# Pooling V for the last twenty head pairs on GpSimd, from a second load of V, and the FFN blocks dealt out four and five to a slot

## The chip, the cores and the metric

The kernel runs on one core of a Trainium2 chip. The core has five engines with a queue of instructions each: TensorE (PE, matrix multiplies, with PEld for its weight loads), VectorE (DVE), ScalarE (ACT), GpSimd (POOL) and SyncE (SP, which here does nothing but issue transfers). Sixteen DMA engines move the data. The metric is the time of one execution on the device, in microseconds (us); the median of several runs is compared.

## What is computed

Local and pooled attention are added, and the sum goes through a gated feed-forward network (FFN). Q, K and V have 8 batches, 8 heads, 576 tokens and 64 columns.

```python
q_d = q.reshape(B, H, Sd, factor, D).mean(axis=3)      # factor = 4, Sd = 144
k_d = k.reshape(B, H, Sd, factor, D).mean(axis=3)
v_d = v.reshape(B, H, Sd, factor, D).mean(axis=3)
out_d = sm_attn(q_d, k_d, v_d)                         # softmax attention over 144 pooled tokens
out_up = np.repeat(out_d, factor, axis=2)
mask = np.abs(pos[:, None] - pos[None, :]) < factor    # a band of seven keys
scores = np.where(mask, scale * np.matmul(q, k.transpose(0, 1, 3, 2)), -1e9)
attn = softmax(scores)
x = (out_up + np.matmul(attn, v)).transpose(0, 2, 1, 3).reshape(B * S, H * D)
return (np.maximum(x @ w_gate, 0.0) * (x @ w_val)) @ w_out   # 4608 x 512, FFN width 1536
```

The change is about `v_d`, the mean of V over each group of four tokens.

## The kernel before

Work on attention goes by **pairs** of heads, 32 of them (`p`), four to a batch. The FFN goes by **chunks** of 512 tokens, nine of them (`c`): twelve h blocks each (eight matmuls into two PSUM banks, a Relu on ACT, a product `g` on DVE, lines 532 to 548) and four y blocks (twelve matmuls into one bank, a copy `y_sb` on ACT, lines 550 to 562). `ffn` (line 571) lists the blocks in order, with the y blocks of chunk c-1 between the h blocks of chunk c: h h h y, and so on; in the first chunk an empty entry stands where a y would be. `ffn_do` (line 580) takes the next entry, but an h block of chunk c is only taken once all pairs of the batches that it reads are done (`made`, at least four times the number of those batches); otherwise it returns with nothing done.

The order of all instructions is written out by hand in `slot(n)` (line 604), which is called for n from -2 to 33. In slot n the pair n has its scores, pair n-1 or n-2 its outputs, and later pairs are loaded and cast; `quota` says how many FFN blocks are dealt into the slot: none before slot 4, three up to slot 13, four from slot 14 on. What is left of `ffn` after the last slot runs as a tail. Every engine works through its own instructions in this order.

The first twelve pairs (`NPE = 12`) are transposed by PE. The last twenty are transposed by DMA: `turn_qk` and `turn_a` on SP's queue (lines 239 and 456). For them a slot has these steps, in program order:

- SP: `turn_a(n-1)` (L459 and L460, which make `at` and `adt`), `turn_qk(n+2)` (L244, twice), then `load` of pair n+5 (Q and K in rows of 256 bytes, L178, into `nat`; V twice into `vst`, L185), then `store_y` (L567).
- PE: `scores(n)` (L313, `s_ps`), `scores_d(n)` (L330, `d_ps`), `pool_v(n)` (L344 and L353, `v_ps`), an FFN block, `outputs(n-2)` (L487 `u_ps`, L504 `o_ps`), and three more FFN blocks.
- DVE: mask (L364), maximum and subtraction (L386, L387, `sm`), the pooled maximum (L370, L371), then the products `g`, the sums and weights of pair n, and `add_x(n-2)` (L521), which adds `u_ps` and `od` into `xT`.
- ACT: `copy_vd(n)` (L397), the exponentials (L418, L406), the Relus, `od` (L512), a cast of Q (L224), `y_sb` (L561).
- POOL: `pool_qk(n+1)` (L300 `t`, L303 `qkd`), `weights_d(n)` (L447 `adn`, two multiplications), and for pair n+3 the cast of K (`cast_qk_pool`, L226) and of V (`cast_v`, L237).

V is loaded so that its tokens lie by windows: a tile `vst` of 112 partitions, rows 0 to 47 and 64 to 111, with 18 windows of 64 columns; it is cast into `v16`. The outputs of the local attention multiply this tile. `pool_v` makes the pooled V from the same tile with a constant matrix `pool_sb` that holds 0.25: eight matmuls (L344) accumulate the first 128 groups of four tokens of both heads into `vp[:, 0:2]`, and four smaller ones (L353) give the last 16 groups, in `vp[:, 2:4]`. `copy_vd` casts the whole to `vd`, which `outputs` multiplies with `adt`.

All of `s_ps`, `v_ps`, `h_ps`, `u_ps`, `o_ps` and `y_ps` come from one pool of six PSUM banks that are given out in turn (`bank`, line 138); `d_ps` has two of its own. The SBUF pools that the change touches are `v16` (7 buffers), `sm` (2) and `vst` (3 fixed tiles, `v_t[p % NV]`).

Of the kernel before, what the change touches and what calls it, by code (L numbers as in the profile page):

```python
# [10 lines left out]
FP32 = mybir.dt.float32  # L11
FP16 = mybir.dt.float16
AF = mybir.ActivationFunctionType
ALU = mybir.AluOpType
# [27 lines left out]
def _dap(t_ap: bass.AP, extra_off: int, dims) -> bass.AP:  # L42
    return bass.AP(tensor=t_ap.tensor, offset=t_ap.offset + extra_off, ap=list(dims))
# [3 lines left out]
def kernel(  # L47
# [10 lines left out]
    nc = tc.nc  # L58
    B, H, S, D = q.shape
# [11 lines left out]
    NPE = 12  # L71
# [16 lines left out]
    def pool(name, bufs):  # L88
        return ctx.enter_context(tc.tile_pool(name=name, bufs=bufs))
# [7 lines left out]
    en_t = [cpool.tile([96, 12, 64], FP16, name=f"en{i}") for i in range(NA)]  # L97
    ad_t = [cpool.tile([80, 6, 128], FP16, name=f"adn{i}")[:, 0:5] for i in range(NA)]
    p_nat = pool("nat", 4)
    p_16 = pool("h16", 3)  # L100
    p_at = pool("at", 2)
    p_adt = pool("adt", 2)
# [11 lines left out]
    nc.scalar.activation(out=warm, in_=warm, func=AF.Exp)  # L114
    nc.scalar.dma_start(mask_sb, mask_dr)
    nc.scalar.dma_start(pool_sb, pool_dr)
    p_v16 = pool("v16", 7)
    p_t1 = pool("t1", 1)
    p_qkd = pool("qkd", 2)
    p_sm = pool("sm", 2)  # L120
    p_e = pool("e", 2)
    p_st = pool("st", 4)
    p_ed = pool("ed", 2)
    p_vd = pool("vd", 4)
    p_od = pool("od", 2)
    psum = ctx.enter_context(tc.tile_pool(name="psum", bufs=6, space=bass.MemoryType.PSUM))
    psum_d = ctx.enter_context(tc.tile_pool(name="psum_d", bufs=2, space=bass.MemoryType.PSUM))
# [10 lines left out]
    def bank(shape, name, dt=FP32):  # L138
        return psum.tile(shape, dt, name=name, tag="bank")


    def load_h_weights(i):
        cols = slice(384 * i, 384 * i + 384)
        for src, dst in ((w_gate, wg_sb), (w_val, wv_sb)):
            nc.gpsimd.dma_start(
                dst[:, :, cols],
                _dap(src, 384 * i, [[DF, 128], [128 * DF, 4], [1, 384]]),
            )

    def load_y_weights(i):  # L150
        nc.gpsimd.dma_start(
            wo_sb[:, 3 * i : 3 * i + 3, :],
            _dap(w_out, 3 * i * 128 * DM, [[DM, 128], [128 * DM, 3], [1, DM]]),
        )


    st = {}

    def load(p):
        off = 2 * p * S * D  # L160
        nat = p_nat.tile([96, 2, 768], FP32, name="nat", tag="nat")
        if p < NPE:


            t = nat.rearrange("p a c -> p (a c)").rearrange("p (b h c) -> p b h c", b=3, h=2)
            for src, r0, r1, blk, g0 in (
                (q, 0, 96, 0, 0),
                (q, 0, 48, 1, 96),
                (k, 48, 96, 1, 0),
                (k, 0, 96, 2, 48),  # L170
            ):
                nc.sync.dma_start(  # L172
                    t[r0:r1, blk],
                    _dap(src, off + 4 * g0 * D, [[4 * D, r1 - r0], [S * D, 2], [1, 4 * D]]),
                )
        else:
            for i, src in ((0, q), (1, k)):
                nc.sync.dma_start(  # L178
                    nat[:, i].rearrange("p (h j d) -> p h j d", h=2, j=6),
                    _dap(src, off, [[D, 96], [S * D, 2], [96 * D, 6], [1, D]]),  # L180
                )
        vst = v_t[p % NV]

        def win(rows, lo, par, w, nw):
            nc.sync.dma_start(  # L185
                vst[64 * par + lo : 64 * par + lo + rows, w : w + nw, :],
                _dap(
                    v,
                    off + (32 * (2 * w + par) - 3 + lo) * D,
                    [[D, rows], [64 * D, nw], [1, D]],  # L190
                ),
            )


        if p == 0:
            win(48, 0, 0, 1, NW - 1)
            win(45, 3, 0, 0, 1)
        else:
            win(48, 0, 0, 0, NW)
        if p == NP - 1:  # L200
            win(48, 0, 1, 0, NW - 1)
            nc.vector.memset(vst[96:VR, NW - 1, :], 0.0)
            win(35, 0, 1, NW - 1, 1)
        else:
            win(48, 0, 1, 0, NW)
        st[p] = dict(nat=nat, vst=vst)


    def cast_qk(p, i):
# [18 lines left out]
    def cast_qk_act(p):  # L228
        cast_qk(p, 0)
# [108 lines left out]
    def pool_v(p):  # L338
        s = st[p]
        v16 = s["v16"]  # L340
        s["vp"] = vp = bank([128, 4, D], "v_ps")
        v2 = v16.rearrange("p (h l) d -> p h l d", h=2)
        for l in range(8):
            nc.tensor.matmul(  # L344
                out=vp[:, 0:2, :],
                lhsT=pool_sb[:, 128 - 16 * l : 256 - 16 * l],
                rhs=v2[:, :, l, :],
                start=(l == 0),
                stop=(l == 7),
            )  # L350
        for c in range(2):
            for h in range(2):
                nc.tensor.matmul(  # L353
                    out=vp[64 * h : 64 * h + 64, 2 + c, :],
                    lhsT=pool_sb[:, 128 - 32 * c : 192 - 32 * c],
                    rhs=v2[:, h, 8, :],
                    start=True,
                    stop=True,
                )
# [34 lines left out]
    def copy_vd(p):  # L394
        s = st[p]
        s["vd"] = p_vd.tile([128, 4, D], FP16, name="vd", tag="vd")
        nc.scalar.copy(out=s["vd"], in_=s.pop("vp"))  # L397

    def exp_d(p, h):
        s = st[p]  # L400
        if h == 0:
            s["ed"] = p_ed.tile([80, 4, S // 4], FP16, name="ed", tag="ed")
            s["sd"] = p_st.tile([80, 4], FP32, name="sd", tag="sd")
        for c in range(2):
            i = 2 * h + c
            nc.scalar.activation(  # L406
                out=s["ed"][:, i, :],
                in_=s["dp"][h][:, c, :],
                func=AF.Exp,
                scale=SCALE / 16.0,  # L410
                bias=s["nb"][:, i : i + 1],
                accum_out=s["sd"][:, i : i + 1],
            )
# [150 lines left out]
    def store_y():  # L564
        while ysb:
            row, y_sb = ysb.pop(0)
            nc.sync.dma_start(_dap(out, row * DM, [[DM, 128], [1, DM]]), y_sb)  # L567
# [12 lines left out]
    def ffn_do():  # L580
        if ffn:
            t = ffn[0]
            if t and t[0] == "h" and made[0] < 4 * (min((t[1] + 1) * TCH - 1, NTOK - 1) // S + 1):
                return
            ffn.pop(0)
            if t:
                (ffn_h if t[0] == "h" else ffn_y)(t[1], t[2])
# [5 lines left out]
    def at_stage(p, *fs, pe=None):  # L593
        if 0 <= p < NP and (pe is None or pe == (p < NPE)):
            for f in fs:
                f(p)
# [5 lines left out]
    loaded = [0]  # L602

    def slot(n):
        quota = 0 if n < 4 else 3 if n < 14 else 4
        at_stage(n - 1, turn_a, pe=False)
        at_stage(n + 2, turn_qk, pe=False)
        while loaded[0] < min(NP, n + (5 if n < NPE - 2 else 6)):
            load(loaded[0])
            loaded[0] += 1  # L610
        store_y()
        at_stage(n, scores, scores_d)
        at_stage(n - 1, turn_en_pe, pe=True)
        at_stage(n, pool_v, mask_l, shift_l, copy_vd, exp_l, max_d)
        if n == 0:
            cast_qk_act(1)
        at_stage(n + 2, cast_qk_pool, pe=True)
        if n + 2 < NPP:
            at_stage(n + 2, cast_v, pe=True)
        at_stage(n + 1, pool_qk, pe=False)  # L620
        if n < 4 or n >= NPE:
            at_stage(n + 1, turn_qk_pe, pe=True)
        if quota > 1:
            ffn_do()
        if 4 <= n < NPE:
            at_stage(n + 1, turn_qk_pe, pe=True)
        at_stage(n - 1, turn_ad_pe, pe=True)
        at_stage(n, lambda p: exp_d(p, 0))
        at_stage(n - 1, outputs, pe=True)
        at_stage(n - 2, outputs, pe=False)  # L630
        at_stage(n, sums, weights_l)
        at_stage(n - 1, x_stage, pe=True)
        at_stage(n - 2, x_stage, pe=False)
        at_stage(n, lambda p: exp_d(p, 1))
        if n != -1:
            at_stage(n + 2, cast_qk_act, pe=True)
        if quota:
            ffn_do()
        if n + 2 >= NPP:
            at_stage(n + 2, cast_v, pe=True)  # L640
        at_stage(n + 1, pool_qk, pe=True)
        at_stage(n, weights_d)
        at_stage(n + 3, cast_qk_act, cast_qk_pool, cast_v, pe=False)
        if 1 <= n < 5:
            load_h_weights(n - 1)
        elif 5 <= n < 9:
            load_y_weights(n - 5)
        if quota > 2:
            ffn_do()
        if quota > 3:  # L650
            ffn_do()

    with tc.manual_schedule():
# [35 lines left out]
```

## Time and profile before

| What | us |
|---|---|
| median of three runs | 412.59 (412.29 to 413.22) |
| the profiled execution | 413.64 |
| its span, from the first to the last instruction | 411.9 |
| PE busy in the span | 388.7 |
| L344, the eight pooling matmuls, 256 in all (mean 234 ns each as recorded, overlapping) | 21.9 |
| POOL busy | 167.8 |
| waits of PE in the slots from 130.48 to 251.52 | none |
| DMA: 59.02 MB, of which HBM read | 42.63 MB |

A line of the chain of waits has the start, the length and the work; the chain is followed back from the last instruction, so its pieces are the time that set the end. A line of a timeline has the start, the length, the engine, the line of the code, the operation, output and inputs, and in brackets how long the engine stood idle before it and for whom it waited. In the table by stretches the columns are the stretch, its length, the busy times of PE, PEld, DVE, ACT and POOL with the number of instructions, the TensorE clock that was granted (1.00 is full), the mean busy share of the sixteen DMA engines (packets overlap, so it can exceed 1), and GB/s. In the page's forty slices each digit is a busy share in tenths. SPq is SP's queue of transfers; the length there is the time that issuing took. Lengths of one engine's instructions overlap a little, since the next starts before the last has drained.

### The profile page before, as it was taken

Reading aid. Unit: us, or ns where it says so; the run is one execution under the profiler, and the core shown is the slowest. Engines: PE = TensorE matmul, PEld = TensorE weight load, DVE = VectorE, ACT = ScalarE, POOL = GpSimd, SP = SyncE. Lnnn points to the kernel's source line nnn. Section 1 sums busy time; section 2 is a strip of 40 time slices with the busy share of each in tenths; the row PEclk is TensorE's granted clock in tenths of the full one; section 3 lists DMA queues with packets and bytes.
Section 4 is the critical chain, followed back from the end, with each engine's and each line's share of the span. In section 5 each row is a group of like instructions: output and inputs, shape, how many; then the busy total and the mean of one; then the engine's idle time right before and its main releaser. Section 6 shows DMA issues by size and latency. Waiting matters only on the chain.

```text
span 411.9 us, 11866 instructions
## 1 busy us (share of the span) xinstructions
PE 388.7 (94%) x4704; PEld 205.6 (50%) x4704; DVE 252.1 (61%) x639; ACT 208.2 (51%) x580; POOL 167.8 (41%) x212
## 2 busy tenths in 40 slices
PE   2699998898999999999999999999999999999996
PEld 2587455454555555455555555545554444444442
DVE  2789599878668777777777777777773232232220
ACT  3577578766665555555555555555442322322321
POOL 5587776655557544444444444444211000000000
PEclk9999999898999999999999999999999999999999
DMA  8999999968996999889989899766341100010012
GB/s 189 235 228 231 239 220 227 204 127 143 195 193 142 191 197 190 163 181 198 182 182 181 180 180 179 165 127 120 52 54 50 44 34 27 34 42 27 27 51 102
DMA packets 167261, 59.02 MB, mean 143 GB/s; under 512 B 149846, under 2 KB 162598, under 8 KB 167206
## 3 DMA queue, kind: packets, MB, share of 16 engines
q1 hardware_dynamic: 161030, 53.38, 64.3%
q0 software_dynamic: 5824, 4.72, 7.8%
q8 instruction: 37, 0.61, 0.7%
q10 hardware_dynamic: 352, 0.16, 0.2%
q14 instruction: 18, 0.15, 0.1%
HBM read 42.63 MB, written 9.44 MB: 126 GB/s over the span
## 4 chain that ended last, share of the span: by engine, by line
PE 77%; DMA 6%; DVE 6%; ACT 4%; SPq 3%; issue 2%; POOL 1%; ACTq 0%; POOLq 0%; DVEq 0%
PE h_ps L537 42%; PE y_ps L553 22%; DMA vst<-in_v_dram 5%; SPq L172 3%; PE v_ps L344 3%; PE o_ps L504 2%; PE s_ps L313 2%; PE u_ps L487 2%; DVE sm L387 2%; PE d_ps L330 1%; DVE s_ps L364 1%; DVE mx L386 1%; DMA nat<-in_k_dram 1%; ACT ed L406 1%; ACT r L545 1%
## 5 line engine op out<-in xcount | busy, mean ns | idle before, releaser
L547 DVE TENSOR_TENSOR g<-r,h_ps 128x512 f16<-128x512 f16 x108 | 74.0, 685 | 120.0 <-PE h_ps L537 116.7
L537 PE MATMUL h_ps<-xT,wg_sb 128*128 128x512 f16 x432 | 114.2, 387 | 0.2 <-DVE xT L521 0.2
L537 PE MATMUL h_ps<-xT,wv_sb 128*128 128x512 f16 x432 | 113.5, 386 | 0.0
L553 PE MATMUL y_ps<-wo_sb,g 128*128 128x512 f16 x432 | 99.5, 382 | 0.0
L447 POOL TENSOR_TENSOR adn<-ed,rd 80x512 f16<-80x512 f16 x64 | 41.1, 662 | 119.1 <-ACT h L224 72.3
L545 ACT ACTIVATE r<-h_ps 128x512 f16<-128x512 f32 x108 | 64.1, 593 | 39.3 <-PE h_ps L537 39.2
L537 PEld LDWEIGHTS <-wv_sb 128*128 128x128 f16 x432 | 42.9, 99 | 53.3 <-issue 3.7
L553 PEld LDWEIGHTS <-g 128*128 128x128 f16 x432 | 42.5, 99 | 51.9 <-issue 1.9
L537 PEld LDWEIGHTS <-wg_sb 128*128 128x128 f16 x432 | 38.3, 99 | 42.2 <-issue 2.7
L561 ACT COPY y_sb<-y_ps 128x512 f32<-128x512 f32 x36 | 21.1, 585 | 75.7 <-PE y_ps L553 75.7
L406 ACT ACTIVATE ed<-d_ps,nb 80x144 f16<-80x144 f32 x128 | 47.5, 381 | 0.0
L237 POOL CAST v<-vst 112x1152 f16<-112x1152 f32 x32 | 36.7, 1147 | 3.7 <-DMA vst<-in_v_dram 3.7
L300 POOL TENSOR_TENSOR t<-qkT 128x576 f32<-128x576 f16 x27 | 31.3, 1158 | 12.6 <-DVE qkT L269 8.9
L418 ACT ACTIVATE e<-sm 96x456 f16<-96x456 f32 x32 | 18.7, 583 | 30.8 <-DVE sm L387 30.7
L226 POOL CAST h<-nat 96x768 f16<-96x768 f32 x35 | 29.7, 847 | 5.0 <-DMA nat<-in_k_dram 5.0
L370 DVE TENSOR_REDUCE d_ps<-d_ps 80x2 f32<-80x288 f32 x64 | 28.9, 452 | 0.0
L397 ACT CAST vd<-v_ps 128x256 f16<-128x256 f32 x32 | 11.9, 373 | 32.8 <-PE v_ps L353 32.8
L521 DVE TENSOR_TENSOR xT<-u_ps,od 128x288 f16<-128x288 f32 x64 | 26.0, 446 | 3.0 <-ACT od L512 3.0
L224 ACT CAST h<-nat 96x768 f16<-96x768 f32 x29 | 24.2, 840 | 4.5 <-DMA nat<-in_k_dram 4.5
L387 DVE TENSOR_TENSOR sm<-s_ps,mx 96x228 f32<-96x228 f32 x64 | 25.1, 392 | 2.2
L406 ACT ACTIVATION_READ_ACCUMULATOR ed<-d_ps,nb 80x1 f32 x128 | 26.3, 205 | 0.0
L364 DVE TENSOR_TENSOR s_ps<-s_ps,mask_sb 96x228 f32<-96x228 f32 x64 | 22.1, 389 | 4.3 <-PE s_ps L313 4.3
(50 smaller groups left out, 367.0 us busy)
## 6 DMA issues: line engine op xcount, KB each, us to landing
vst<-in_v_dram SPq DMA_DIRECT2D x62, 216.0 KB, 5.0
out_dram<-y_sb SPq DMA_DIRECT2D x36, 256.0 KB, 2.2
nat<-in_q_dram SPq DMA_DIRECT2D x20, 288.0 KB, 3.4
nat<-in_k_dram SPq DMA_DIRECT2D x20, 288.0 KB, 4.3
nat<-in_q_dram SPq DMA_DIRECT2D x12, 192.0 KB, 6.3
nat<-in_k_dram SPq DMA_DIRECT2D x12, 192.0 KB, 5.3
wg_sb<-in_moe_w_gate_dram POOLq DMA_DIRECT2D x4, 384.0 KB, 7.7
wv_sb<-in_moe_w_val_dram POOLq DMA_DIRECT2D x4, 384.0 KB, 10.5
```

Of the source, the lines that this page charges most:

```text
L226: nc.gpsimd.tensor_copy(out=dst, in_=src)
L237: nc.gpsimd.tensor_copy(out=s["v16"], in_=s.pop("vst"))
L300: nc.gpsimd.tensor_tensor(out=t1, in0=qkv[:, :, :, 0], in1=qkv[:, :, :, 1], op=ALU.add)
L364: nc.vector.tensor_tensor(out=sp, in0=sp, in1=mask_sb, op=ALU.add)
L370: nc.vector.tensor_reduce(out=nbr, in_=s["dp"][h], axis=AX.X, op=ALU.max)
L387: nc.vector.tensor_tensor(out=sm[:, half, :], in0=sp, in1=mx[:, half, None].to_broadcast([96, 6, 38]), op=ALU.subtract,)
L406: nc.scalar.activation(out=s["ed"][:, i, :], in_=s["dp"][h][:, c, :], func=AF.Exp, scale=SCALE / 16.0, bias=s["nb"][:, i : i + 1], accum_o ...
L447: nc.gpsimd.tensor_tensor(out=o, in0=i, in1=rd[:, :, None].to_broadcast([80, 4, n]), op=ALU.mult)
L537: nc.tensor.matmul(out=h, lhsT=w[:, kk, bass.ts(jj, 128)], rhs=xT[:, kk, bass.ts(c, TCH)], start=(kk == 0), stop=(kk == 3),)
L545: nc.scalar.activation(out=r, in_=h1, func=AF.Relu)
L547: nc.vector.tensor_tensor(out=g, in0=r, in1=h2, op=ALU.mult)
L553: nc.tensor.matmul(out=y, lhsT=gts[c][jj][:, bass.ts(ty, 128)], rhs=wo_sb[:, jj, :], start=(jj == 0), stop=(jj == NJJ - 1),)
```

## The change

For the last twenty pairs, V is loaded a second time by `load_v4`: 128 partitions, each with a group of four tokens of both heads, in rows of 4 x 64 floats (1 KB). `sum_v4` adds the four tokens on POOL in two steps, and `copy_vd` scales the sum by 0.25 on ACT into `vd[:, 0:2]`. The eight matmuls of `pool_v` (L344) are left out for these pairs; the four of the last 16 groups stay, and their copy is an instruction of its own.

The other load of V is taken out of `load` into `load_v`. For the last twenty pairs it stands in slot n for pair n+4 instead of n+5, after the loads of Q and K and ahead of `load_v4`; `cast_v` moves from pair n+3 to n+2. The number of `v16` buffers goes from 7 to 5, of `sm` from 2 to 1; new are three buffers of `v4` and three of `s4`. From slot 14 on `quota` is four in even slots and five in odd ones.

```diff
+    p_v4 = pool("v4", 3)
...
-    p_v16 = pool("v16", 7)
+    p_v16 = pool("v16", 5)
...
-    p_sm = pool("sm", 2)
+    p_sm = pool("sm", 1)
...
+    p_s4 = pool("s4", 3)
...
+    def load_v4(p):
+        st[p]["v4"] = v4 = p_v4.tile([128, 2, 4 * D], FP32, name="v4", tag="v4")
+        nc.sync.dma_start(
+            v4, _dap(v, 2 * p * S * D, [[4 * D, 128], [S * D, 2], [1, 4 * D]])
+        )
+
+    def sum_v4(p):
+        s = st[p]
+        v4 = s.pop("v4")
+        s2 = v4[:, :, 0 : 2 * D]
+        nc.gpsimd.tensor_tensor(out=s2, in0=s2, in1=v4[:, :, 2 * D : 4 * D], op=ALU.add)
+        s["s4"] = p_s4.tile([128, 2, D], FP32, name="s4", tag="s4")
+        nc.gpsimd.tensor_tensor(
+            out=s["s4"], in0=s2[:, :, 0:D], in1=s2[:, :, D : 2 * D], op=ALU.add
+        )
...
-        for l in range(8):
+        for l in range(8) if p < NPE else ():
             nc.tensor.matmul(
                 out=vp[:, 0:2, :],
...
-        nc.scalar.copy(out=s["vd"], in_=s.pop("vp"))
+        vp = s.pop("vp")
+        if p < NPE:
+            nc.scalar.copy(out=s["vd"], in_=vp)
+        else:
+            nc.scalar.copy(out=s["vd"][:, 2:4], in_=vp[:, 2:4])
+            nc.scalar.activation(
+                out=s["vd"][:, 0:2], in_=s.pop("s4"), func=AF.Copy, scale=0.25
+            )
...
-        quota = 0 if n < 4 else 3 if n < 14 else 4
+        quota = 0 if n < 4 else 3 if n < 14 else 5 if n % 2 else 4
...
             load(loaded[0])
+            if loaded[0] < NPE:
+                load_v(loaded[0])
             loaded[0] += 1
+        at_stage(n + 4, load_v, load_v4, pe=False)
         store_y()
...
-        at_stage(n + 3, cast_qk_act, cast_qk_pool, cast_v, pe=False)
+        at_stage(n + 3, cast_qk_act, cast_qk_pool, pe=False)
+        at_stage(n + 2, cast_v, sum_v4, pe=False)
...
         if quota > 3:
+            ffn_do()
+        if quota > 4:
             ffn_do()
```

More of the change, by code (lines that the diff above doesn't have):

```diff
@@ L181, in load, with load_v @@
                 )
+        st[p] = dict(nat=nat)
+    def load_v(p):
+        off = 2 * p * S * D
         vst = v_t[p % NV]
@@ L205, in load @@
             win(48, 0, 1, 0, NW)
-        st[p] = dict(nat=nat, vst=vst)
+        st[p]["vst"] = vst
+    def load_v4(p):
[12 more added lines that the diff above has]
+        )
     def cast_qk(p, i):
```

## The prediction

> **What bounds the kernel now.** I read the page first, then the chain of waits, then single slots in the timelines.
>
> ```profile
> PE 388.7 (94%) x4704; PEld 205.6 (50%) x4704; DVE 252.1 (61%) x639; ACT 208.2 (51%) x580; POOL 167.8 (41%) x212
> PE   2699998898999999999999999999999999999996
> DMA  8999999968996999889989899766341100010012
> ```
>
> PE is full from about the twelfth slice on; up to slice 26 the DMA engines are nearly full too, and after that almost idle. So there are two candidates for the late slots, PE and transfers. The chain of waits from 241 to 252 us decides between them. It shows slot 25 (each pair has a slot, numbered here by its scores; T is the start of its `s_ps`, here 241.43):
>
> ```profile
> 241.43 0.36 PE s_ps L313 x36
> 241.79 0.25 PE d_ps L330 x4
> 242.04 0.55 PE v_ps L344 x8
> 242.59 0.18 PE v_ps L353 x4
> 242.77 1.83 PE h_ps L537 x8
> 244.60 0.39 PE u_ps L487 x36
> 245.00 0.37 PE o_ps L504 x8
> 245.37 1.83 PE h_ps L537 x8
> 247.20 2.59 PE y_ps L553 x12
> 249.79 1.73 PE h_ps L537 x8
> 251.52 0.36 PE s_ps L313 x36
> ```
>
> Every piece is PE and each begins where the last ended: a slot is PE work alone, 10.09 us. The slots from 130.48 on repeat this to 0.01 us. Its four blocks are h (1.73 us, 1.83 right after small matmuls) or y (2.59), and the tail after 320 us is the same blocks back to back. What PE loses in these slots comes off the end, if nothing else becomes late.
>
> **Part 1, eight pooling matmuls removed for pairs 12 to 31.** 0.55 us a slot in the row of L344; its four companions of L353 stay. Slots 13 to 31 are pure PE. In slot 12 the chain names DVE, but there PE runs s, d, v, then a y block (115.15 to 117.75); ACT stood idle 0.86 us before it copied that y (117.95) and made `adt` (118.44), for which `o_ps` waited 0.49 us. So v lies on the path there too. 20 x 0.55 = **-11.0 us**.
>
> **Part 2, five blocks in the odd slots.** By the block list, a slot runs what is ready, and chunk c waits until 4(c+1) pairs are done. That allows 29 blocks before slot 14 in both kernels, then 80 in before; in after the chunks 6 and 7 are not ready in slots 28/29 and 32/33, so 87, and the tail falls from 39 to 32 blocks. A block costs PE the same in a slot as in the tail: 0. Only the 0.10 us of an h after small matmuls falls away where a y or nothing stands there, up to ten times: between 0 and -1.0, taken as **-0.5**, the middle.
>
> **Part 3, banks that come free too late.** PE now comes to everything after v_ps 0.55 us sooner, while DVE's chain does not. The six PSUM banks go in turn (s s v h h u u o h h y ...), each to the sixth next user. The same slot on DVE:
>
> ```profile
> 243.16 0.39 DVE L387 TENSOR_TENSOR sm<-s_ps,mx 96x228 f32<-96x228 f32 x1
> 243.89 0.39 DVE L387 TENSOR_TENSOR sm<-s_ps,mx 96x228 f32<-96x228 f32 x1
> 247.48 0.81 DVE L521 TENSOR_TENSOR xT<-u_ps,od 128x288 f16<-128x288 f32 x2
> ```
>
> The second `sm` frees its bank for `o_ps` at 244.28 = T+2.85; `o_ps` starts at T+3.57 now and T+3.01 after: 0.1 us to spare after a hand-over of 0.05. Thin, but no wait. Where the second and third block of a slot are both h (slots 18 to 21, 26 to 31), the third's second half needs the bank of the first `u_ps`, free at 247.89 = T+6.46; PE comes at 0.79+1.83+0.76+1.83+0.86 = T+6.07. In 20, 21, 28, 30 and 31 the slot before ended in a y, so DVE has no g ahead of its masks and is some 0.2 earlier: a wait of 0.22 x 5 = **+1.1** (none to 0.44 each: 0 to +2.2). Slots 18, 19, 26 and 27 have a y first, which makes PE later, and wait nothing. Slot 29 has no first block at all (chunk 6 isn't ready): PE runs into the banks of `s_ps` (0.3) and then of `u_ps` (1.1): **+1.4** (0 to +2).
>
> **Part 4, GpSimd.** Two adds a pair over 128x256 and 128x128. L300 takes 1158 ns for 576 elements and L303 725 for 288: 1.50 ns an element and 0.29 fixed, so 0.68 + 0.48 = 1.16 us. POOL is busy 4.92 us of a 10.09 us slot (windows by slot); 6.1 of 9.54 still fits. Queued behind the adds are t and qkd of the next pair: qkd ends at 254.10, and the scores that need it start at 261.96. Hidden: 0; without that cover 20 x 1.16 = 23 us.
> [...]
>
> **Part 5, small moves.** ACT's copy of vd (256 wide, 373 ns) becomes two of 128; the nearest row is `od`, 144 wide, 275 ns: +0.17 us, in a gap of 1.1 us before `e`. `sm` with one buffer: it is written again 8.3 us after `e` has read it. V's load and cast keep their distance of two slots, one slot later; v16 of five is enough as the outputs of pair p-5 end 6 us before the cast of p. All 0.
>
> **Part 6, one more transfer per slot, the doubtful one.** SP issues nine transfers a slot in order and has hardly a pause:
>
> ```profile
> 132.42 1.23 SPq L459 DMA_TRANSPOSE at<-en  x1
> ...
> 250.17 0.57 SPq L178 DMA_DIRECT2D nat<-in_q_dram  x1
> 250.79 0.59 SPq L178 DMA_DIRECT2D nat<-in_k_dram  x1
> 251.49 1.82 SPq L185 DMA_DIRECT2D vst<-in_v_dram  x2
> 253.72 1.88 SPq L567 DMA_DIRECT2D out_dram<-y_sb  x1
> 255.71 1.24 SPq L459 DMA_TRANSPOSE at<-en  x1
> ```
>
> L459 ends at 133.65 in slot 14 (T+3.17) and 256.95 in slot 26 (T+5.43): SP's round takes 123.3/12 = 10.28 us, a little more than the slot. It slides back, and nothing feels it yet, for `at` must land (4.0 us after issue, median) only for `u_ps` of the next slot. The new transfer (256 KB, rows of 1 KB) adds at least an issue of 0.43 (L172's transfers of 1 KB rows) and a gap of 0.09, 0.52; at most 256 KB at the 183 GB/s of these slots, 1.42. From the y stores of the tail (0.08 busy over 60 us, 7.7 stores of 128 packets: 77 ns a packet of 2 KB) 256 packets cost each of 16 engines between 0.62 and 1.23, middle 0.92. I take 0.52, because the slots that SP passes without a stretched issue take 9.3 to 9.9 us (213.46 to 222.92, for one), so SP mostly issues and isn't held by the engines. A round is then 10.80. PE's slots with loads (14 to 27) take 9.54 with four blocks and 11.2 to 12.0 with five, mean 10.49. SP falls back 0.31 x 14 = 4.3 us. It starts at T+4.4 (3.17, plus the new transfer, plus slot 13 being 0.55 shorter) and is too late at T+9.4 (9.54 + 2.62 for `u_ps`, less 2.8): 5.0 us of room. **0**, with 0.7 to spare. In slots 8 to 12 five new transfers (2.6 to 4.6 us) fall before SP's pause from 84.65 to 93.35, which hides them; without it that is their price. Behind the new transfer on SP wait y's store and the next `at`; the other load of V, one slot later, moves its two issues past no deadline.
>
> **The clock.**
>
> ```profile
> 96.80:100.31 3.51, 2.28 (x54) 1.51 (x52) 3.37 (x9) 3.51 (x14) 1.17 (x2) 1.00 0.87 198
> 100.31:103.72 3.41, 3.41 (x9) 1.22 (x8) 1.89 (x5) 1.39 (x4) 1.73 (x2) 0.50 1.27 227
> ```
>
> After 3.5 us with PE busy for 2.28 (second column), the next 3.41 us run at half clock (third from the end): 1.7 us lost. It happens once more at 79.83, after 2.80 of 4.42. Slot 29 now gets a similar idle share: 0 to +1.7, taken as 0, since other stretches (116 to 120, 3.51 of 4.00) passed.
> [...]
>
> **Sum.** -11.0 - 0.5 + 1.1 + 1.4 = -9.0 on the span of 411.9, to 402.9. The profiled execution took 413.64, 1.74 more than its span, and lies 1.05 above the median of 412.59; the same -9.0 from the median is **403.6**. Own range: from -11.0 - 1.0 and a little bank waiting, 401.3, to -11.0 with waits of 2.5 and 1.7 of clock and a few tenths, 405.5.
>
> **Rivals.**
> *SP a little too slow.* At 0.92 a round is 11.20: 0.71 x 14 = 9.9, less 5.0 of room, PE waits 4.9: 408.5. For it: four of twelve rounds take 10.6 to 11.8, with stretched issues behind V's loads. Against: the engines' share is 0.96 in these slots and was 1.20 from 20 to 60 us.
> *Slower than before: transfers bound the loading slots.* At 1.42 a round is 11.70: 1.21 x 14 = 16.9, less 5.0, +11.9: 415.5. It ends slower from a round of 10.49 + 14.0/14 = 11.49, an added 1.21. For it: SP already needs 10.28. Against: the byte price treats rows of 1 KB like the 256-byte rows of Q, K and V.
> *The gain goes into the bank of `o_ps`.* If DVE's `sm` came 0.3 us later, `o_ps` would wait 0.2 in the ten slots with an h first behind an h, and the other bank waits double: 2.0 + 2.5, 408.1. DVE's rows in the slots are steady to 0.01 us, against it; POOL's new adds run beside that chain, for it.
> *The eight matmuls were hidden anyway:* no change, 412.6; the chain has them end to end.
>
> **How the numbers follow.** Forecast 0.63, SP a little slow 0.17, bank 0.09, slower 0.09, hidden 0.02. About 0.2% can be told from no change. Faster 0.89, same 0.02, slower 0.09. The range 401.3 to 408.0 holds the forecast and a good half of the two middle rivals.
>
> **What would show it.** No L344 after about 111 us; slots of 9.5 and 11.2 to 12.0 us in turn; PE idle only near slot 29. Wrong, if `u_ps` waits for DMA `at<-en` from slot 20 on (SP), if `o_ps` waits for DVE `sm` (bank), or if POOL's adds take over 2 us.

## The result, and the profile after

| | us | runs | ratio to before |
|---|---|---|---|
| before, beside after | 412.35 (408.70 to 415.31) | 20 | |
| after | **410.02** (405.34 to 413.04) | 20 | 0.9922 (95%: 0.9895 to 0.995) |
| forecast | 403.6 (401.3 to 408.0) | | |

The kernel became faster by 2.3 us, not by 9.0; the range was missed by 2.0. The ratios leave out the runs more than 1.5% above the fastest of the same kernel (4 of after's 20); since the runs of one kernel spread here over as much as 9 us, the medians of all runs stand beside them in this text.

The profiled execution of after took 405.34, the fastest of its twenty runs, against 413.64 for the one of before: 8.3 less, which looks like the forecast come true. It isn't. First the page of after, rows of section 1, 2 and 5:

```profile
PE 375.6 (93%) x4544; PEld 196.4 (49%) x4544; DVE 253.2 (63%) x639; ACT 210.4 (52%) x600; POOL 191.5 (47%) x252
PE   2699998898999999999999998999699999999996
DMA  7999999998999999999999899898831100100012
...
L568 PE MATMUL h_ps<-xT,wg_sb 128*128 128x512 f16 x432 | 113.1, 384 | 3.0 <-DVE xT L552 3.0
```

The 160 matmuls are gone (4544 for 4704), and PE is busy 13.1 us less. But the row of PE, which was full from the twelfth slice to the end, now has an 8 in slice 25 and a 6 in slice 29 (282 to 293 us), and the h blocks (L537 before, L568 now) wait 3.0 us for DVE's `xT`.

A fair comparison needs the part of the run that the change touches. I take the stretch from the start of pair 12's `s_ps` to the end of the last matmul. The timeline of PE, in before:

```profile
113.55 0.43 PE L313 MATMUL s_ps<-qkT 64*32 64x38 f16 x36
...
403.83 4.05 PE L553 MATMUL y_ps<-wo_sb,g 128*128 128x512 f16 x18
```

and in after:

```profile
108.85 0.43 PE L336 MATMUL s_ps<-qkT 64*32 64x38 f16 x36
...
395.69 4.05 PE L584 MATMUL y_ps<-wo_sb,g 128*128 128x512 f16 x18
```

In before the stretch is 403.83 + 4.05 - 113.55 = 294.33 us (ends rounded), in after 399.73 - 108.85 = 290.88: 3.45 us less. Another 4.7 us (113.55 to 108.85) lie ahead of slot 12, where PE's work is the same. There the profile of before has two windows of 3.4 us at half clock (79.8 and 100.3 us, 1.7 us lost in each); the profile of after has neither, but the profile of the same kernel in e11 has both (78.1 and 98.5), and its slot 12 starts at 112.25. So the one execution flatters the change by 3.4 us (and by another 1.3 in slot 4), and the stretch doesn't. It is given for every run below.

Where the stretch lost what was forecast is seen at slot 29 (T = 283.25), again in PE's timeline of after:

```profile
283.86 0.25 PE L377 MATMUL v_ps<-v,pool_sb 112*64 112x64 f16 x4
285.01 0.46 PE L518 MATMUL u_ps<-at,v 38*64 38x32 f16 x36 [0.90 <-DMA at<-en]
285.46 0.44 PE L535 MATMUL o_ps<-adt,vd 128*64 128x80 f16 x8
285.97 0.82 PE L568 MATMUL h_ps<-xT,wg_sb 128*128 128x512 f16 x3
289.28 0.58 PE L568 MATMUL h_ps<-xT,wg_sb 128*128 128x512 f16 x1 [2.49 <-DVE xT L552]
289.66 1.91 PE L568 MATMUL h_ps<-xT,wv_sb 128*128 128x512 f16 x4
```

Two different waits. `u_ps` waits 0.90 for the transpose `at`: SP is late. Then the first h block of chunk 6 stops after three matmuls for 2.49 us. A wait for a bank would stop the first matmul of a block; this one stops the fourth. The first three read the columns of x that three of the batch's pairs made; the fourth reads those of pair 27, whose addition has not yet been made. DVE's timeline shows why:

```profile
287.60 0.23 DVE L456 RECIPROCAL rl<-sl 96x12 f32<-96x12 f32 x1
287.86 0.63 DVE L461 TENSOR_TENSOR en<-e,rl 96x456 f16<-96x456 f16 x1
288.41 0.81 DVE L552 TENSOR_TENSOR xT<-u_ps,od 128x288 f16<-128x288 f32 x2
```

The addition (L552) stands last in DVE's chain of the slot, at T+5.16. And the clock falls behind the wait; the two windows of the table by stretches:

```profile
285.40:288.80 3.40, 1.32 (x22) 0.61 (x12) 3.23 (x11) 2.29 (x10) 1.29 (x3) 1.00 1.05 81
288.80:292.20 3.40, 2.92 (x7) 0.99 (x7) 0.95 (x3) 0.60 (x1) 1.81 (x2) 0.50 0.73 219
```

PE was busy 1.32 of 3.40 us, and in the next 3.40 us its clock is 0.50.

Slots 25 and 29 pay for SP's lateness. Slot 25 in PE's timeline, and a round of SP with the transfers of the second load (L217):

```profile
242.76 0.46 PE L518 MATMUL u_ps<-at,v 38*64 38x32 f16 x36 [0.70 <-DMA at<-en]
243.68 0.44 PE L535 MATMUL o_ps<-adt,vd 128*64 128x80 f16 x8 [0.46 <-DMA adt<-adn]
```

```profile
226.78 1.27 SPq L490 DMA_TRANSPOSE at<-en  x1
228.16 1.22 SPq L491 DMA_TRANSPOSE adt<-adn  x1
229.47 2.55 SPq L267 DMA_TRANSPOSE qkT<-h  x2
232.07 0.57 SPq L180 DMA_DIRECT2D nat<-in_q_dram  x1
232.69 0.58 SPq L180 DMA_DIRECT2D nat<-in_k_dram  x1
233.37 3.18 SPq L191 DMA_DIRECT2D vst<-in_v_dram  x2
236.65 1.00 SPq L217 DMA_DIRECT2D v<-in_v_dram  x1
237.74 0.41 SPq L598 DMA_DIRECT2D out_dram<-y_sb  x1
238.29 1.32 SPq L490 DMA_TRANSPOSE at<-en  x1
```

From one `at` to the next SP takes 11.51 us here, without a pause. From the end of `at` in slot 14 (129.16, T+4.46) to that in slot 27 (273.38, T+11.92) it is 144.22/13 = **11.09 us a round**; the same two points of before give 10.29. PE's thirteen slots are 10.52 on average. SP so falls back by 7.5 us where it may fall back by 5.

### The profile page after: what moved, and what is told of

The parts are those of the page before. It is cut to its first block, busy times and chain, and to the rows that moved or that the text cites. A ratio compares the mean times of both kernels' runs of the same rounds, so it can differ in the third digit from the quotient of the medians.

```text
span 403.5 us, 11622 instructions
## 1 busy us (share of the span) xinstructions
PE 375.6 (93%) x4544; PEld 196.4 (49%) x4544; DVE 253.2 (63%) x639; ACT 210.4 (52%) x600; POOL 191.5 (47%) x252
## 4 chain that ended last, share of the span: by engine, by line
PE 77%; ACT 7%; DVE 6%; DMA 4%; issue 3%; POOL 2%; SPq 1%; ACTq 0%; POOLq 0%
PE h_ps L568 42%; PE y_ps L584 23%; PE o_ps L535 2%; PE s_ps L336 2%; ACT ed L437 2%; PE u_ps L518 2%; PE d_ps L353 2%; DVE sm L411 2%; DMA nat<-in_k_dram 1%; PE t_ps L283 1%; DVE s_ps L388 1%; DVE mx L410 1%; PE t_ps L304 1%; PE v_ps L377 1%; ACT r L576 1%
## 5 line engine op out<-in xcount | busy, mean ns | idle before, releaser
L568 PE MATMUL h_ps<-xT,wg_sb 128*128 128x512 f16 x432 | 113.1, 384 | 3.0 <-DVE xT L552 3.0
L568 PE MATMUL h_ps<-xT,wv_sb 128*128 128x512 f16 x432 | 112.4, 383 | 0.0
L568 PEld LDWEIGHTS <-wv_sb 128*128 128x128 f16 x432 | 42.6, 99 | 55.4 <-issue 5.5
L584 PEld LDWEIGHTS <-g 128*128 128x128 f16 x432 | 41.6, 98 | 49.2
L568 PEld LDWEIGHTS <-wg_sb 128*128 128x128 f16 x432 | 38.9, 99 | 43.6 <-issue 1.9
L552 DVE TENSOR_TENSOR xT<-u_ps,od 128x288 f16<-128x288 f32 x64 | 26.0, 446 | 5.0 <-ACT od L543 5.0
L461 DVE TENSOR_TENSOR en<-e,rl 96x456 f16<-96x456 f16 x32 | 23.9, 747 | 1.1
```

The source lines that it names most:

```text
L568: nc.tensor.matmul(out=h, lhsT=w[:, kk, bass.ts(jj, 128)], rhs=xT[:, kk, bass.ts(c, TCH)], start=(kk == 0), stop=(kk == 3),)
L584: nc.tensor.matmul(out=y, lhsT=gts[c][jj][:, bass.ts(ty, 128)], rhs=wo_sb[:, jj, :], start=(jj == 0), stop=(jj == NJJ - 1),)
```

## The experiments

Each row gives the medians of all runs, the ratio, the stretch and SP's round as above (from the profiled execution), PE's idle time from slot 11 on in it (waits over 0.05 us), and the median of the granted clock over the runs. "Ready" is the dealing of e5.

| | kernel | us (runs) | ratio (95%) | stretch | idle | round | clock |
|---|---|---|---|---|---|---|---|
| | before, beside e11 to e14 | 412.34 (35) | | 294.33 | 0.68 | 10.29 | 0.991 |
| e8 | before, ready dealing | 412.76 (11) | 1.0005 (0.9976 to 1.0034) | 294.33 | 0.68 | 10.47 | 0.990 |
| e4 | before, dealing of after | 418.73 (6) | 1.0153 (1.0106 to 1.02) | 299.72 | 4.26 | 10.54 | 0.988 |
| | after, as above | 410.02 (20) | 0.9922 (0.9895 to 0.995) | 290.88 | 5.84 | 11.09 | 0.984 |
| e1 | after | 412.16 (6) | 0.9858 (0.9771 to 0.9946) | 290.50 | 5.45 | 10.99 | 0.983 |
| e11 | after | 410.07 (12) | 0.9957 (0.9919 to 0.9994) | 291.39 | 5.46 | 10.99 | 0.983 |
| e3 | after, four blocks in every slot | 415.34 (12) | 1.0092 (1.0056 to 1.0129) | 298.18 | 11.08 | 10.95 | 0.988 |
| e2 | after, no second load | 409.54 (12) | 0.9922 (0.9889 to 0.9956) | 290.88 | 4.92 | 10.33 | 0.982 |
| e5 | after, ready dealing | 407.02 (5) | 0.9885 (0.984 to 0.993) | 289.19 | 4.05 | 11.04 | 0.991 |
| e12 | the same | 408.24 (12) | 0.992 (0.9885 to 0.9955) | 291.47 | 7.43 | 11.11 | 0.992 |
| e6 | ready, no second load | 404.43 (5) | 0.9801 (0.9756 to 0.9845) | 284.23 | 1.05 | 10.29 | 0.990 |
| e9 | ready, second load on GpSimd's queue | 409.94 (11) | 0.9879 (0.984 to 0.9917) | 292.53 | 7.13 | 11.20 | 0.990 |
| e13 | ready, second load between the transposes | 409.37 (12) | 0.9893 (0.9842 to 0.9944) | 290.22 | 4.88 | 11.16 | 0.990 |
| e10 | ready, y's stores on GpSimd's queue | 409.17 (9) | 0.9889 (0.9839 to 0.9939) | 284.41 | 1.46 | 10.55 | 0.989 |
| e14 | the same | 407.50 (12) | 0.9856 (0.9811 to 0.99) | 287.34 | 4.05 | 10.88 | 0.988 |
| e7 | ready, y's stores on ACT's queue | 412.21 (11) | 0.9958 (0.9917 to 1.0) | 293.21 | 7.20 | 10.56 | 0.986 |

**e1, after unchanged.**

> The changed kernel again, for a second profile and the granted clock of every run beside that of the kernel before. SP theory (SP's round of transfers takes about 11.0 us against 10.5 us of PE work in a loading slot, so `at` and `adt` come late and PE stands still, more in some executions than in others): a profile with more PE idle time in the slots from 20 on than the 5.8 us after 100 us of the first profile, at `u_ps` and `o_ps`, and half-clock windows right behind the stalls; median 408 to 411. Rival, low activity of the shorter slot alone lowers the clock: half-clock windows where PE has not stalled.

412.16 in the median of six, again far from 403.6, with a quick profiled run (404.82) as before. Its stretch, 290.50, is after's to 0.4; its ratio rests on two of the six. So after's shortfall is no accident of one set of runs.

**e2, the second load left out.** Three fixed tiles, filled once with zeros by DVE, stand in for the loaded ones, so the pooled V of these pairs is zero; the additions on GpSimd stay.

```diff
-    p_v4 = pool("v4", 3)
+    v4_t = [cpool.tile([128, 2, 4 * D], FP32, name=f"v4_{i}") for i in range(3)]
...
-        st[p]["v4"] = v4 = p_v4.tile([128, 2, 4 * D], FP32, name="v4", tag="v4")
-        nc.sync.dma_start(
-            v4, _dap(v, 2 * p * S * D, [[4 * D, 128], [S * D, 2], [1, 4 * D]])
-        )
+        st[p]["v4"] = v4_t[p % 3]
```

> Leaves out the second load of V: GpSimd adds the same two steps over three tiles filled with zeros once, so the pooled V of the last twenty pairs is zero there. SP theory: the round falls back to 10.1 to 10.3 us, below PE's 10.5, nothing is late: 403 to 405 against 412.4 before, clock of every run at 0.99 or above. Rivals (bank waits behind DVE, GpSimd's adds, the dealing of blocks, the clock by itself): unchanged, 408 to 411.

The round falls to 10.33 and no `u_ps` waits for a DMA, yet the stretch is 290.88, to 0.01 that of after, and the ratio is after's too, 0.9922: not the 403 to 405 of the SP theory, but the 408 to 411 of its rivals. The waits of PE in that stretch:

```profile
PE h_ps L567 <- DVE xT L551: 3.5, 3, 2.8
PE o_ps L534 <- DVE sm L410: 0.7, 1, 0.7
PE o_ps L534 <- ACT adt L508: 0.5, 1, 0.5
```

The columns are the sum, the number and the longest of the waits. Slot 29 has grown: 2.85 us for `xT` where after has 2.49, 0.73 for a bank, and 6.8 us at half clock behind them. What SP's lateness took from PE in after, slot 29 takes here: PE's idle time is 0.9 us less than in after, and one more window runs at half clock.

**e3, four blocks in every slot, and the load.**

```diff
-        quota = 0 if n < 4 else 3 if n < 14 else 5 if n % 2 else 4
+        quota = 0 if n < 4 else 3 if n < 14 else 4
```

> The changed kernel with four blocks in every slot from 14 on. SP theory: PE's slot is 9.54 us and SP's round 11.0, so 14 slots lose 1.46 each, 20 us less some 5 of room: 15 us lost of 11 won, 414 to 418. Bank rival (five blocks cause the waits): faster than the change, 401 to 403.

This is slower than before. With slots of 9.53 us SP, at 10.95, sets the pace, and `u_ps` waits 8.3 us for `at`, in six places. The five-block slots of the change are therefore needed: they give SP time.

**e4, only the dealing, in before.** The same line the other way, and a fifth `ffn_do()`.

> The kernel before, with only the dealing of four and five blocks in turn. SP theory: the mean loading slot becomes 11.0 us of PE work against a round of 10.3, so SP no longer falls back; PE has the same work: 411 to 412.5, with fewer low-clock runs than before if late transfers cause them there too. Bank rival: 413 to 415, waits at the third h block of a slot.

6.1 us slower than the 412.67 of before beside it, with no second load and no missing matmul: the strongest single loss of the study. Slot 29 in PE's timeline, and its two windows:

```profile
297.23 0.82 PE L537 MATMUL h_ps<-xT,wg_sb 128*128 128x512 f16 x3
301.15 0.59 PE L537 MATMUL h_ps<-xT,wg_sb 128*128 128x512 f16 x1 [3.10 <-DVE xT L521]
```

```profile
297.60:301.00 3.40, 0.46 (x3) 0.10 (x1) 3.26 (x10) 2.30 (x10) 0.04 (x1) 1.00 1.08 121
301.00:304.40 3.40, 3.25 (x8) 1.16 (x8) 0.88 (x3) 0.60 (x1) 0.00 (x0) 0.51 0.19 43
```

The same fourth matmul, the same wait, the same half clock behind it. The cause is the dealing: of the 5.4 us that the stretch is longer than before's, 3.6 are added idle time, and 3.25 us of work at a clock of 0.51 lose 1.6. Neither expectation had it (411 to 412.5, 413 to 415).

**e5 and e8, no block dealt ahead of its rows**, in after and in before. Slots 25, 27 and 31 deal four blocks and slot 32 three, so that chunk 5 still has blocks when slot 29 begins.

```diff
-        quota = 0 if n < 4 else 3 if n < 14 else 5 if n % 2 else 4
+        quota = 0 if n < 4 else 3 if n < 14 or n == 32 else 5 if n % 2 and n not in (25, 27, 31) else 4
```

> The changed kernel with four blocks instead of five in slots 25, 27 and 31 and three in slot 32, so that two blocks of chunk 5 and 4 are still there for slot 29 and the first h of chunk 6 comes after the sum of pair 27 has been written. Data theory (slot 29 starts chunk 6 while DVE has not yet added pair 27 into its rows; 2.5 us of waiting and 3.4 to 6.8 us at half clock behind it): no wait before the first h of chunk 6, 3.5 to 5 us gained on the change, 405 to 406.5, if the transfers, which now have 4 us less of PE work above them, don't take 1 to 3 us of it back (407 to 408). SP theory alone: slower than the change, 411 to 413.

> The kernel before with the same new dealing. Data theory: the 6 us that four and five blocks in turn cost the kernel before go away, 411.5 to 413. If five blocks in a slot cost it by themselves (banks, DVE): still 415 to 419.

In before the loss of e4 is gone to the last hundredth (294.33, as before itself). In after the wait of 2.49 us and the half clock behind it are gone too, but slot 25 has become short, `u_ps` waits 1.12 and 1.62 us for `at` in slots 26 and 27, and a half-clock window stands behind these (269.5).

**e6, both costs taken away.** e5 with the edit of e2.

> Both causes taken away: the dealing of the run before, and no second load of V (leaves it out; the pooled V of the last twenty pairs is zero there). Data and SP theory together: PE busy without a wait over 0.5 us from 122 us on, 400 to 402.5, granted clock of the runs like that of the kernel before (0.99). If the clock falls by itself in these shorter slots: 404 to 408 at a clock of 0.985 or less.

284.23, 10.10 less than before: what the eight matmuls were worth. PE is idle 1.05 us from slot 11 on, 0.68 of it as in before. The other 0.37 is the wait of slot 29 in small, at the fourth matmul of the first h block of chunk 5 (slot 25) and of chunk 6 (slot 29):

```profile
251.31 0.81 PE L567 MATMUL h_ps<-xT,wg_sb 128*128 128x512 f16 x3
252.31 0.38 PE L567 MATMUL h_ps<-xT,wg_sb 128*128 128x512 f16 x1 [0.19 <-DVE xT L551]
```

Slot by slot against e8, which has the same dealing, fifteen of the twenty slots are shorter by 0.55 or 0.56 us, slot 12 by 0.45, slots 20 and 21 by 0.47 each, and slots 25 and 29 by 0.21 each. In the medians the gain is less, 8.5 us beside the 412.89 of before (21 runs), and 404.4 lies above the expected 400 to 402.5. There are only five runs, and what lies ahead of slot 12 counts in them: in this profile slot 4, whose work is the same, took 13.76 us, in the other fifteen 10.7 to 12.5.

**e7, y's stores on ACT's queue**, with the dealing of e5.

```diff
-            nc.sync.dma_start(_dap(out, row * DM, [[DM, 128], [1, DM]]), y_sb)
+            nc.scalar.dma_start(_dap(out, row * DM, [[DM, 128], [1, DM]]), y_sb)
```

> The dealing of the run before last, and the stores of y issued from ACT's queue, so that SP has one transfer less a slot. If SP's issuing is what takes 11 us a round: the round falls to 10.2 to 10.4, lateness shrinks, 402 to 404. If the DMA engines are what takes it: the round stays at 10.8 to 11.2, and the time is that of the same dealing with the stores on SP, 405 to 408.

It doesn't answer its question, for its round, 10.56, lies between its two cases, and it makes a wait of its own. SP's queue, where Q and K of one pair are loaded:

```profile
97.27 1.13 SPq L180 DMA_DIRECT2D nat<-in_q_dram  x1
108.24 0.31 SPq L180 DMA_DIRECT2D nat<-in_k_dram  x1
```

Between the two SP stands for 9.8 us. The load of K at 108.24 starts 3.12 us after a store of y which ACT issued at 105.12, and such stores take 2.9 us to land (median): most likely a store of y that waits on ACT so stops a load on SP until it has landed. The rows don't name what the load waited for; a likely cause, not tested, is that both wait on one completion semaphore, for in the packed trace of after the 290 transfers of SP and the three of ACT's queue carry the same eight. A second such stop (126.4 to 131.1, where the load starts 3.24 us after a store issued at 127.83) costs PE 3.49 us at slot 14.

**e9, the second load on GpSimd's queue.**

```diff
-        nc.sync.dma_start(
+        nc.gpsimd.dma_start(
             v4, _dap(v, 2 * p * S * D, [[4 * D, 128], [S * D, 2], [1, 4 * D]])
         )
```

> The kernel of e5 (slot 29 deals three blocks fewer, so that no block is dealt before its rows), and the second load of V is issued from GpSimd's queue instead of SP's; every transfer and every sum stays. What is asked is what makes SP's round 11.09 us with the second load: SP's own issuing of it, or the 16 DMA engines that move its 256 KB. If it is the issuing (my theory now): SP's round falls back to 10.3 us or so, the end of the transpose `at` stays at most 4.5 us behind the start of the slot, u_ps waits for no DMA in slots 20 to 31, and the time is 404 to 405.5 us, as without the load (404.4). If the DMA engines set it: the round stays near 11 us, the lag grows to 10 us or more as in e5, and the time is 407 us. [...]

My theory of SP's issuing fell. One issue less, and the round is not shorter but 11.20. From the loads of one round of SP in e9 to the next `at` (this round has two stores of y):

```profile
207.55 0.57 SPq L180 DMA_DIRECT2D nat<-in_q_dram  x1
208.18 1.40 SPq L180 DMA_DIRECT2D nat<-in_k_dram  x1
209.67 2.16 SPq L191 DMA_DIRECT2D vst<-in_v_dram  x2
211.87 1.47 SPq L598 DMA_DIRECT2D out_dram<-y_sb  x2
213.45 1.24 SPq L490 DMA_TRANSPOSE at<-en  x1
```

and in e6, which has no second load at all:

```profile
211.27 0.58 SPq L182 DMA_DIRECT2D nat<-in_q_dram  x1
211.90 0.60 SPq L182 DMA_DIRECT2D nat<-in_k_dram  x1
212.60 1.88 SPq L193 DMA_DIRECT2D vst<-in_v_dram  x2
214.57 0.69 SPq L597 DMA_DIRECT2D out_dram<-y_sb  x1
215.38 1.26 SPq L489 DMA_TRANSPOSE at<-en  x1
```

The issues that stayed on SP have become longer. Summed over thirteen rounds, the loads of Q, K and V's first load take 4.40 us a round in e9, 3.37 in e5 and 3.17 in e6; the second load's own row in e5 is 0.80. The time left SP's row L217 and came back in the others. Another issuer so saved SP's round nothing: 11.20 against 11.04 in e5. Nor does pooled V come late: GpSimd's issue of the load takes 0.74 us, and no matmul of e9 waits for GpSimd. But e9 changes more than the issuer: from 130 to 270 us, thirteen of these loads went as 1040 packets on GpSimd's queue, and in e5 as 3328 packets on SP's.

**e10, y's stores on GpSimd's queue.** The edit of e7 with `nc.gpsimd`.

> The kernel of e5, with the stores of y issued from GpSimd's queue instead of SP's; the second load of V stays on SP. It takes 0.41 us of a row of issuing from SP's round for each store and leaves all bytes on the DMA engines. If SP's issuing sets the round (my theory): 11.09 falls to about 10.6 us, the lag of `at` ends at 5 to 7 us instead of 12, the waits of u_ps of 1.1 and 1.6 us in e5 are gone or under 0.3 us, and the time is 404.5 to 406 us. If the DMA engines set it: the round stays at 11 us and the time at 407 us. If GpSimd's queue is the dearer one (its store waits for y_sb ahead of the adds that pool V): the adds move later, u_ps waits for them, and the time is over 407 us.

Profile and time disagree. The profiled run is as expected: a round of 10.55, one wait over half a microsecond, a stretch of 284.41, nearly e6's. But it is the fastest of nine runs (403.44); the median is 409.17, where the third case has it, though in the profile no matmul waits for GpSimd.

**e11 to e14, four kernels in turn on one chip**: after, e5's kernel, the second load elsewhere in SP's order, and e10's kernel. The edit of e13, in `slot`:

```diff
         at_stage(n - 1, turn_a, pe=False)
+        at_stage(n + 3, load_v4, pe=False)
         at_stage(n + 2, turn_qk, pe=False)
...
-        at_stage(n + 4, load_v, load_v4, pe=False)
+        at_stage(n + 4, load_v, pe=False)
```

> The kernel after, unchanged, on the same chip and in turn with the next three, because its runs lie between 404.8 and 413.6 us and those of e5, e9 and e10 came from other calls. My theory (the dealing of slot 29 costs 3 to 5 us, the second load's lateness 2 to 3): 410 to 412.5 us, 3 to 5 above e12. If the difference between after and e5 was one of chip and hour: no more than 1.5 us between this and e12.

> The kernel of e5 once more (slot 29 deals three blocks fewer, and nothing else differs from after). My theory: 406.5 to 408 us, and less than e11 by 3 to 5. If e5's 407.0 came from five lucky runs: 409 us or more.

> e12 with the second load of V issued elsewhere in SP's order: between the transposes adt and qkT of a slot (for pair n+3) instead of behind the loads of Q, K and V (for pair n+4). Every byte and every issue stays on SP. e9 left two readings of the 11.09 us round. If the load costs SP its own issue only, in any place (issuing): the round and the time are e12's, 407. If the cost lies in the pile of loads, where the engines have most to move and hold SP's next issue back (rows of V's first load of 1.9 to 3.2 us, of K's load of 0.6 to 1.7): outside of it the round falls to 10.5 to 10.8 us, the lag of `at` ends under 9 us, and the time is 405 to 406.5. If the transposes behind it suffer instead (qkT later, so that t of the next pair is late on GpSimd): s_ps or the masks wait, over 408.

> e10 once more (stores of y on GpSimd's queue), beside e12: its nine runs lay between 403.4 and 411.1 us, and the profile of the fastest had no late `at`. If SP's relief lasts in every run (my theory of issuing): 404 to 406.5 and 1 to 2.5 us below e12. If it only moves the lateness into other runs: 408 to 410, not below e12.

e12 against e11 is 1.8 us (1.5 by the ratios), less than the 3 to 5 that I expected, and in these two profiles the stretch is the same (291.47 and 291.39): with the second load in place, the ready dealing mostly trades slot 29's wait for later transfers. Over all runs the kernel of e5 and e12 has 407.4 (17 runs) and after 410.1 (38): 2.7. In e12 the lateness reaches further than `u_ps`:

```profile
PE u_ps L518 <- DMA at<-en: 3.3, 4, 1.5
PE h_ps L568 <- ACT y_sb L592: 1.8, 1, 1.8
```

The 1.8 us are a block that waits for ACT to copy an earlier y. y's stores stand behind the loads on SP; the likely reason, not tested, is that a late store keeps its buffer.

e13: between the transposes the load's own row falls to 0.57, but the loads of Q and K grow to 1.68 us a round (1.37 in e5), and the round is 11.16. The case with the lower round fell. The first case has the round and, within the noise, the time of e12 (ratios 0.9893 and 0.992), but an issue of 0.57 doesn't make the 0.87 by which the round is longer than e6's. e14: a round of 10.88 and 407.50, 0.7 below e12, between its two cases. Three places, on two queues, for the same 256 KB give a round of 11.0 to 11.2: the cost goes with the load, whichever row it shows in. It doesn't follow that SP's issuing counts for nothing, for without y's stores the round is 10.55 to 10.88 (e7, e10, e14). And whether the sixteen DMA engines are the limit stays open: their mean busy share from 140 to 240 us is 0.97 in e5 and 0.95 in e9, but 1.02 in e6, which has no second load.

## Why the prediction was wrong, point by point

**Part 1, right; Part 2, without its half microsecond.** e6 has a stretch 10.10 us shorter than before's, where eight matmuls times 20 were put at 11.0. The 0.55 us are there in fifteen of the twenty slots; the 0.9 that is missing lies in slots 25 and 29, which lose 0.34 each to the wait for `xT` (0.19 and 0.18 of it recorded as idle), and in slots 12, 20 and 21, about 0.1 each. That a block costs PE the same in a slot as in the tail holds in e8, whose stretch is before's; nothing of the -0.5 shows there or in e4.

**Part 3, slot 29: the step that failed, with the clock.** I said that slot 29 has no first block because chunk 6 isn't ready, and priced what follows as waits for two banks, 0.3 and 1.1. The place was right, the wait was not. The bank of `s_ps` did cost PE 0.73 us in e2 and e11, but the next wait is for data: chunk 6 becomes ready within slot 29, when pair 27's outputs are issued, and its fourth matmul needs the addition at the end of DVE's chain. I had taken a block that the list calls ready as one whose rows are there. It is 2.49 us in after, 2.85 in e2, 3.10 in e4, 1.98 in e11; the first h block of chunk 7, in slot 33, waits 0.48 in the same way. And the clock, which I left at 0 with 1.7 as bound, came: one window of 3.4 us at half clock in the profile of after, 6.8 us in e2's and e11's. The step alone costs 5.4 us of the stretch in before (e4 against e8) and 6.7 in after without the load (e2 against e6), 6.0 and 5.1 in the medians, for a forecast of 1.4.

**Part 6, the second load: mis-sized.** The shape was right: SP starts at T+4.46 (forecast 4.4), falls back slot by slot, and the first wait, in slot 25, follows an `at` that ended at T+9.77 of slot 24 (forecast 9.4). The size was not: I took the shortest issue, 0.52, for a round of 10.80, because SP "mostly issues and isn't held by the engines". It is 11.09, an added 0.80; the middle bound, 0.92 and a round of 11.20, was nearer. In after the load's own issue is 0.86 us a round, where 0.43 was taken from the row of L172, and the other rows together are no longer than in before; in e9 and e13 it is the others that grow. The sign that the prediction named for this, `u_ps` waiting for `at` from slot 20 on, came in slots 25 and 29. The lateness alone (e5 and e12 against e6) costs 5.0 and 7.2 us of the stretch and 3.0 in the medians (407.4 against 404.4), for a forecast of 0.

**The two losses cover each other.** That is what neither the forecast nor the rivals had. From e6's 284.23, the dealing alone adds 6.7, the load alone 5.0 to 7.2, and both together, in after, 6.3 to 7.2. The 0.90 us that `u_ps` waits in slot 29 would be waited for DVE anyway; the 1.16 of slot 25 are balanced, in the profiles of after and e1, by a half-clock window less in slot 29 than in e2 (e11 has both windows, and 291.39); and the five-block slots 25 and 27, which use up chunk 5 too early, are the same that give SP some 2 us more each. So taking away one part alone brings 0.5 us in the medians (e2, not told apart from none) or 2.7 (e5 and e12), taking away both 5.7.

**The clock as a whole.** The median of the granted clock is 0.984 in after's runs and 0.982 in e2's, but 0.991 in before's and 0.992 in e12's. 0.007 of 410 us is 2.9 us, and it goes with the dealing, not with the load; in before the same dealing gives 0.988 (e4).

**The rest.** GpSimd's additions took 0.72 and 0.45 us (forecast 0.68 and 0.48):

```profile
229.43 0.72 POOL L225 TENSOR_TENSOR v<-v 128x256 f32<-128x256 f32 x1
230.23 0.45 POOL L227 TENSOR_TENSOR s<-v 128x128 f32<-128x128 f32 x1
```

and no matmul of after waited for them: hidden, as said. Of the five bank waits of 0.22, 1.1 together, none shows at the place that was named, the second half of the third block. In after slots 20, 21 and 28 are longer than the others of their length by 0.22, 0.09 and 0.14 us, and that lies at `u_ps`. The rival of SP being a little too slow (408.5) had the right mechanism and nearly the right round, and gave 4.9 us for it; it had no slot 29. The slower side (415.5) is what e3 became once the five-block slots were away, by the same mechanism; that 415.34 is the same number is chance, for the round was 10.95 against slots of 9.53, not 11.70 against 10.49. The own range's upper end, 405.5, doesn't follow from its terms: -11.0, 2.5 of waits and 1.7 of clock give 405.8 from the median, before the few tenths.

**Sum, as it came out,** in medians: 412.3 before, less 7.9 without the matmuls and with neither loss (e6: 404.4), plus 3.0 for the second load (e5, e12: 407.4), plus 2.7 for the dealing on top of it (1.5 by the ratios of e11 and e12): 410.1.

**What stays open.** What in the chip makes SP's round longer with the load (under e13), and why the kernel with y's stores on GpSimd's queue runs between 402.2 and 411.1: its two profiles have rounds of 10.55 and 10.88, and which of the transfers differ between executions wasn't found. Over all 21 runs it has 407.9, not told apart from e5's kernel with 407.4. Both are 2 to 3 us below after and 4 to 5 below before, and are the best that keep all of the computation.

## What to carry to other kernels

"Ready" in a list of work that is written out by hand means issued, not computed: before a block is dealt, look where on the other engine's chain the last row that it reads is made, and put an independent block in between. A transfer added to a queue that has no pause is not priced by the shortest issue in the profile but by what it does to the round; here that was 0.80 us where 0.52 was forecast, and moving it to another queue didn't help (11.20 against 11.04 to 11.11). Judge such a change by a stretch that holds only what was changed, and by many runs: the single profile gave 8.3 us for a change worth 2.3.

## What the runs showed of the hardware that was not expected

- The clock fell to half after windows in which PE was far from idle: after 1.32 busy of 3.40 us in after, 1.42 in e2 and 2.38 in e11. In e2 and e11 the next window, itself slowed, has PE busy 1.80 and 1.42 of 3.40, and a second one at half clock follows. A wait of 2.9 us so cost up to 2.6 more: half of the 1.80 + 3.40 that PE works in e2's two windows. Three windows of e2:

```profile
284.50:287.90 3.40, 1.42 (x42) 0.72 (x29) 3.23 (x11) 2.08 (x10) 2.89 (x4) 1.00 0.62 92
287.90:291.30 3.40, 1.80 (x5) 0.68 (x5) 1.51 (x4) 1.15 (x5) 0.00 (x0) 0.50 0.39 121
291.30:294.70 3.40, 3.40 (x10) 1.16 (x9) 0.77 (x2) 0.60 (x1) 1.90 (x3) 0.50 0.00 0
```

- Not every such wait is followed by half clock: e5's of 1.62 us at 268.18 is (the window at 269.5), but e12's of 1.77 us is not, and its profiled execution has a clock of 1.00 throughout:

```profile
213.02 1.02 PE L568 MATMUL h_ps<-xT,wg_sb 128*128 128x512 f16 x4 [1.77 <-ACT y_sb L592]
```

- Two half-clock windows near 79 and 99 us come and go from one execution of the same kernel to the next. Seven of the 35 runs of before had a clock of 1.00 and took 408.2 to 409.6; the others took 411.2 to 414.5.
- The issue of one and the same transfer has no fixed length: that of K took 0.57 us on average in e6 and 0.59 in e5, but 1.16 in e9 (1.40 in the round above), where GpSimd's queue moves 256 KB a round beside it.
